# One gated unit of the second half moved into quads 16 to 18, and the first blocks of attention's output fetched a quad later

## The chip, the cores and the metric

The kernel runs on one core of one Trainium2 chip. The metric is the device time of one execution in microseconds, the median over several runs. Engines are named as in the profile: PE multiplies matrices (PEld is its loading of weights), DVE, ACT and POOL are the vector, scalar and general-purpose engines, and SP issues DMAs only. POOL and ACT issue DMAs too; each of the three has a DMA queue of its own, and 16 DMA engines serve them all.

## The reference, cut to what matters

The input x has 2048 rows of 640 features. The result mixes two branches of it with a gate g per row:

```
g   = sigmoid((x * gate_w).sum(-1))
a   = attention with a compressive memory(x) @ wo          # branch A
b   = (silu(x @ w1) * (x @ w3)) @ w2                       # branch B, inner width 1728
out = g * a + (1 - g) * b
```

Branch A has 32 heads of 20 features and works in 4 chunks of 512 rows. In a chunk every head computes a causal softmax of q k' times v, and beside it reads a memory M (sums of phi(k)' v over the earlier chunks) as phi(q) M / (phi(q) z + 1e-6). Both are mixed per head with sigmoid(beta), and the memory is updated. All is float32; the kernel splits float32 into two parts, so that one product takes three matmuls.

## The kernel before, in words

There are two streams of work for PE, and the Python code that writes the program lays one into the other. PE's order is that of the code; the other engines' order is chosen by the framework's scheduler, except where `here(...)` pins an instruction.

The first stream is attention (`attention`, L752 on). A quad is four heads of one chunk; there are 32, eight to a chunk, numbered 0 to 31, and quads 16 to 23 belong to chunk 2. The time of one quad is cut into 40 slots. Each quad has two visits. The big visit, at slot 5, does the first scores of the new quad (`s_fill`, tiles s, L590), the transposed scores of the quad before it (`t_fill`, tiles t, L623, whose exponentials ACT writes into P, L629) and the product with v of the quad two back (`pv_quad`, tile o, L643). The small visit, at slot 17, does the rest of s and t. In time, "visit O16" below is the big visit in which the o tile of quad 16 is made.

Before t can be computed for a quad, the maximum of each score row is needed: DVE takes the maxima of s (L597), ACT and DVE split them and transpose them (`max_rows`, L608), and two DMAs on ACT's queue write them into two rows of the quad's operand (tile mr into qk, L611). They are issued some slots after the small visit, and the t matmuls of the next big visit wait for them.

The second stream is everything else, in jobs: projections q, k and v of a chunk, reads of the memory (nd, L340), gated units (`ffn_up`, g and u, L262, 15 matmuls for each of g and u and each chunk), down-projections (f, L543), and the output projection of attention (`oproj`: first `normalize`, tiles rr, gt, L717 and L722, then op, L793). Chunks 0 and 1 are the first half, A; chunks 2 and 3 the second, B. `chain`, `braid` and `weave` put jobs after and into each other. Jobs are grouped into segments, `segs`, each with an end in units of ten slots. `begin` takes the next segment and divides its cost by the slots left until its end; the main loop deals out that much of it in each slot, and more of it just ahead of a visit while PSUM banks are held. A segment that is used up early lets the next one begin.

Three things around the change depend on the order. `load_memory` (L705, tile gm) issues four DMAs on POOL's queue that bring back what the memory read stored; it reuses the large buffer in which phi(q) of chunk 2 lies, so for chunk 1 it can only start when the last nd matmul of chunk 2 has read that. `load_pair` (L567, tile qk) issues DMAs on POOL's queue for the next quad's q and k. `o_load` (L690, L692, tile oall) issues DMAs on SP's queue that bring attention's output back, in five blocks of 128 features; `OUT` says after which quad of a chunk which blocks are fetched. PSUM has 8 banks, which `bank_tile` hands out in turn, so that a visit may have to wait until DVE or ACT has read what stood in a bank.

The lines that matter for the time of dealing are these:

```
end, seg = segs.pop(0)
n = end * 10 + LEAD - slots
return [end, (d for _, g in seg for d in g), sum(c for c, _ in seg) * 1e3 / n]
```

Of the kernel before, what the change touches and what calls it, by code (L numbers as in the profile page):

```python
# [18 lines left out]
S, D, H, DH, NSEG, L = 2048, 640, 32, 20, 4, 512  # L19
# [9 lines left out]
NP, AGE = 3, 4  # L29
LAG = 5  # L30
EARLY = range(2, 6)
OUT = {4: (0,), 5: (1,), 6: (2, 3)}
TOP = 1.0e10
HEADS = [(128 * b // DH, min(H - 1, (128 * b + 127) // DH)) for b in range(KB)]
PSEG = ((0, 512), (512, 384), (1024, 256), (896, 128))
# [3 lines left out]
def gated_mix(ctx: ExitStack, tc: tile.TileContext, xT, wqk, wv, w13, w2, w2h, wo, beta, out):  # L39
# [110 lines left out]
    def big_tile(name, dt=F32):  # L150
        return sp.tile([P, 4 * H * VE], dt, tag="big", name=name, bufs=1)
# [174 lines left out]
    def memory_read(c):  # L326
        pq = big.pop(("q", c))[:, :KB * L].rearrange("p (b n) -> p b n", b=KB)
        for qb in range(4):
            for hf in range(2):
                gm = f_tile(f"gm{c}_{qb}_{hf}")[:, :320]  # L330
                ps = bank_tile(f"nd{c}_{qb}_{hf}")
                nd = ps[:, :16 * VE].rearrange("p (h e) -> p h e", e=VE)
                todo = []
                for b in range(KB):
                    a0, a1 = HEADS[b]
                    u0, u1 = max(a0, 16 * hf), min(a1, 16 * hf + 15)
                    if u0 <= u1:
                        todo.append((b, a0, u0, u1))
                for n, (b, a0, u0, u1) in enumerate(todo):
                    nc.tensor.matmul(nd[:, u0 - 16 * hf:u1 - 16 * hf + 1, :],  # L340
                                     pq[:, b, qb * P:(qb + 1) * P],
                                     Ms[c - 1, b][:, u0 - a0:u1 - a0 + 1, :],
                                     start=n == 0, stop=n == len(todo) - 1, skip_group_check=True)
                r = sp.tile([P, 16], F32, tag="r16", name="nd_r")
                nc.vector.scalar_tensor_tensor(r, nd[:, :, DH], 1e-6, gH[:, 16 * hf:16 * hf + 16], op0=ALU.add, op1=ALU.mult)
                nc.vector.reciprocal(r, r)
                nc.vector.scalar_tensor_tensor(
                    gm.rearrange("p (h e) -> p h e", e=DH), nd[:, :, :DH], gate[:, c, 1, qb:qb + 1],
                    r.unsqueeze(2).broadcast_to([P, 16, DH]), op0=ALU.mult, op1=ALU.mult)
                store_later(gd[c][:, qb, 320 * hf:320 * hf + 320], gm, ("g", c, qb), n=2)  # L350
                yield 700
# [102 lines left out]
    def job_read(c):  # L454
        return 5.6, memory_read(c)
# [5 lines left out]
    def job_q(cs, mb, alloc={}):  # L461
        i = w_add(wqk[mb], D)
        return [(3.5, q_block(c, mb, i, alloc.get(c))) for c in cs]

    def job_q2(cs, mb, alloc={}):

        i = w_add(wqk[mb], D)
        j = w_add(wqk[mb + 1], D)
        return [(3.5, q_block(c, m, k, alloc.get(c), j if c == cs[-1] and m > mb else i))
                for c in cs for m, k in ((mb, i), (mb + 1, j))]  # L470
# [14 lines left out]
    def plan_down(js):  # L485
        return [w_add(w2[j] if j < NF else w2h, D) for j in js]
# [41 lines left out]
    def ffn_down(cs, js, idx, last=()):  # L528
        first = js[0] == 0
        w2s = [w_get(i, idx[0]) for i in idx]  # L530
        for c in cs:
            if c in last:
                load_share(c)
            if first:
                accs[c] = slot(f"acc{c}")[:, :KB * L].rearrange("p (b n) -> p b n", b=KB)
            for fb in range(KB):
                ps = bank_tile(f"f{c}_{js[0]}_{fb}", 1300 if len(js) > 2 else 690)
                ms = []
                for j, w in zip(js, w2s):
                    for a, b in (PASSES if j < NF else ((0, 0), (0, 1))):  # L540
                        ms.append((w[:, b, fb * P:(fb + 1) * P], hts[c, j][:, a, :]))
                for n, (w, h) in enumerate(ms):
                    nc.tensor.matmul(ps, w, h, start=n == 0, stop=n == len(ms) - 1)  # L543
                    if n % 3 == 2 and n < len(ms) - 1:
                        yield 699.0 if n == 2 and len(ms) > 5 else 699
                filled()
                dst = accs[c][:, fb]
                if first:
                    nc.scalar.copy(dst, ps)
                elif c not in last:  # L550
                    nc.vector.tensor_add(dst, ps, dst)  # L551
                else:
                    finish(c, fb, ps, (c, fb) == (NSEG - 1, KB - 1))
                yield 699 if len(ms) % 3 == 0 else 466
# [83 lines left out]
    def pv_quad(p):  # L638
# [11 lines left out]
        q = p // 2 % 8  # L650
        for b in OUT.get(q, ()):
            after(8, o_load, c, b)
# [47 lines left out]
    def load_memory(c):  # L700

        assert ("g", c, 3) in stored
        gms[c] = big_tile(f"gm{c}", FR)[:, :KB * L].rearrange("p (b n) -> p b n", b=KB)
        for qb in range(4):
            here(nc.gpsimd.dma_start(gms[c].bitcast(F32)[:, :, qb * P:(qb + 1) * P],  # L705
                                     gd[c][:, qb].rearrange("p (b n) -> p b n", b=KB)))
            yield 1
# [24 lines left out]
    def after(n, f, *a):  # L732
        soon.append([n, f, a])
# [77 lines left out]
    def job_up(cs, j):  # L811
        return (4 if j < NF else 2) * 3.5, ffn_up(cs, j, plan_up([j])[0])
# [6 lines left out]
    def job_down(cs, g, last=()):  # L819
        return 2.32 * sum(3 if j < NF else 2 for j in GROUPS[g]), ffn_down(cs, GROUPS[g], plan_down(GROUPS[g]), last)  # L820

    def jobs_up(cs, g):
        return [job_up(cs, j) for j in GROUPS[g]]
# [4 lines left out]
    def jobs_oproj(c):  # L828
        a, b = oproj(c, plan_wo())
        return (3.5, a), (17.5, b)  # L830
# [10 lines left out]
    def chain(jobs):  # L841
        return sum(c for c, _ in jobs), (y for _, g in jobs for y in g)

    def braid(a, b, every, skip=0, rest=True):

        def gen():
            n = 0
            for y in a[1]:
                yield y
                n += not isinstance(y, float)  # L850
                if n > skip and (n - skip) % every == 0:
                    z = next(b[1], None)
                    if z is not None:
                        yield z
            if rest:
                yield from b[1]
        return a[0] + b[0], gen()

    A, B = (0, 1), (2, 3)
# [15 lines left out]
    segs = []  # L875

    seg = job_q2(A, 3)
# [5 lines left out]
    o1, o2 = jobs_oproj(0)  # L883
    seg = [d, braid(chain(u), o1, 5), o2] + [job_up(A, j) for j in GROUPS[3][2:]] + [job_down(A, 3)]
# [9 lines left out]
    seg = job_q(B, 1) + job_q(B, 2)  # L894
    q = job_q2(B, 3)
    r = job_read(2)
    up = [job_up(B, 0), job_up(B, 1)]
    seg += q[:2] + [braid(chain(q[2:]), r, 2, 7, False)]
    r = 0.6 * r[0], r[1]
    seg += [braid(braid(up[0], r, 2), (0, load_memory(1)), 3, 10)]  # L900
    segs.append((2 * H + LAG + 2, seg))
    up.append(job_up(B, 2))
    o1, o2 = jobs_oproj(1)
    seg = [braid(chain(up[1:]), o1, 4, 11), braid(o2, job_read(3), 3, 1), job_down(B, 0), braid(chain(jobs_up(B, 1)), (0, load_memory(2)), 5)]
    segs.append((3 * H + LAG + 1, seg))
    d = job_down(B, 1)
    u = [job_up(B, j) for j in GROUPS[2][:2]]
    o1, o2 = jobs_oproj(2)
    seg = [d, braid(chain(u), o1, 5), o2] + [job_up(B, j) for j in GROUPS[2][2:]]
# [3 lines left out]
    o1, o2 = jobs_oproj(3)  # L913
# [118 lines left out]
```

## Time and profile before

| | us |
|---|---|
| median of 3 runs | 1116.88 (1114.8 to 1116.93) |
| profiled execution, its time | 1114.77 |
| profiled execution, its span | 1113.0 |
| PE busy | 1096.1 |
| PE mean granted clock over the span | 0.997 |
| DVE, POOL, ACT busy | 587.6, 494.9, 461.9 |

The profile covers one execution, so sums are made against 1114.77; 1.8 us of it lie outside the span. Busy shares are averages over the span. What matters here is a stretch from about 603 to 815 us, quads 13 to 22. There the o matmuls of the visits O13 to O22 start at 603.0, 634.2, 657.8, 685.7, 707.9, 729.8, 749.7, 772.2, 794.7 and 814.8 us; each of these is a PE row of the timeline with the tile o. A row of the timeline gives the start, the duration, the engine, the line, the operation with its tiles, and in brackets the idle time before it with what ended it. Successive matmuls overlap, so a group's cost is the distance between starts.

### The profile page before, as it was taken

The page shows a single profiled execution, that of the slowest core. Times are in us where ns is not written, and L with a number is a line of the kernel's source. Part 1 is how long each engine was busy: PE and PEld are TensorE (multiplying, and loading weights), DVE is VectorE, ACT ScalarE, POOL GpSimd, SP SyncE. Part 2 cuts the span into 40 slices and gives each one's busy share as a digit, 9 for nine tenths or more (in the row PEclk, how much of TensorE's full clock was granted, in tenths as well). Part 3 has the DMA queues.
Part 4 walks back from the last instruction along what each step waited for, and adds up shares of the span by engine and source line. Part 5 has one row for each costly group of instructions (what it writes and reads, how often), then busy time and mean ns, then how long its engine had stood idle before and what let it go on. Part 6 is the DMA issues. An engine that isn't in the chain of part 4 may idle for free.

```text
span 1113.0 us, 17965 instructions
## 1 busy us (share of the span) xinstructions
PE 1096.1 (98%) x6285; PEld 853.2 (77%) x6285; DVE 587.6 (53%) x1708; ACT 461.9 (41%) x952; POOL 494.9 (44%) x603
## 2 busy tenths in 40 slices
PE   9999999999999999999999998999999999999997
PEld 6988877777777777788977776777777777777786
DVE  5032564355565554466253676874557765651545
ACT  6265344454243233265265644435544443344130
POOL 5053445355355254253253436544744445354132
PEclk9999999999999999999999999999999999999999
DMA  8265943335265134446285867454754434432123
GB/s 320 94 232 201 276 116 93 82 89 135 58 147 125 52 84 128 118 105 188 94 270 201 300 185 175 107 161 133 177 127 109 123 83 114 101 104 76 51 59 114
DMA packets 87545, 153.20 MB, mean 138 GB/s; under 512 B 11584, under 2 KB 25184, under 8 KB 87456
## 3 DMA queue, kind: packets, MB, share of 16 engines
q1 hardware_dynamic: 63040, 106.30, 30.1%
q0 software_dynamic: 20384, 38.68, 15.7%
q10 hardware_dynamic: 4032, 7.08, 1.9%
q8 instruction: 50, 0.82, 0.3%
q14 instruction: 39, 0.32, 0.1%
HBM read 96.56 MB, written 54.54 MB: 136 GB/s over the span
## 4 chain that ended last, share of the span: by engine, by line
PE 87%; issue 3%; DMA 3%; DVE 3%; ACT 2%; POOL 2%; SPq 0%; ACTq 0%; DVEq 0%; POOLq 0%
PE g L262 16%; PE f L543 16%; PE u L262 15%; PE v L373 6%; PE k L262 6%; PE q L262 6%; PE o L643 6%; PE s L590 4%; PE op L793 4%; PE t L623 3%; PE pm L437 1%; PE nd L340 1%; DMA qk<-mr 1%; ACT P L629 1%; POOL W L117 1%
## 5 line engine op out<-in xcount | busy, mean ns | idle before, releaser
L117 POOL TENSOR_TENSOR W<-wr,W 128x640 fp32r<-128x640 f32 (+1 forms) x126 | 198.0, 1578 | 280.8 <-ACT W L116 218.7
L597 DVE CUSTOM_DVE_ANT_0 junk<-s,mask 128x256 bf16<-128x256 f32 (+3 forms) x512 | 250.4, 489 | 110.5 <-PE s L590 78.1
L629 ACT ACTIVATE P<-t 128x512 f32<-128x512 f32 (+1 forms) x384 | 172.2, 538 | 144.8 <-PE t L623 115.9
L262 PE MATMUL g<-X,W 128*128 128x512 f32 x840 | 208.6, 398 | 1.6 <-ACT P L629 1.6
L262 PE MATMUL u<-X,W 128*128 128x512 f32 x780 | 197.1, 399 | 0.0
L543 PE MATMUL f<-ht,W 128*128 128x512 f32 x820 | 196.4, 396 | 0.0
L262 PEld LDWEIGHTS g<-X,W 128*128 128x128 f32 x840 | 156.1, 188 | 38.3 <-ACT P L629 1.8
L633 POOL TENSOR_SCALAR_AFFINE_SELECT P<-P 128x256 f32<-128x256 f32 x192 | 93.2, 495 | 198.3 <-ACT P L629 198.1
L543 PEld LDWEIGHTS f<-ht,W 128*128 128x128 f32 x820 | 152.7, 188 | 36.4
L262 PEld LDWEIGHTS u<-X,W 128*128 128x128 f32 x780 | 143.8, 188 | 34.5 <-ACT P L629 0.3
L116 ACT CAST W<-wr 128x640 fp32r<-128x640 f32 (+1 forms) x133 | 95.7, 729 | 128.5 <-PE u L262 28.6
L117 POOL TENSOR_TENSOR ht<-ft,ht 128x512 fp32r<-128x512 f32 x52 | 68.4, 1316 | 82.6 <-ACT ht L116 79.1
L567 POOL DMA_DIRECT2D qk<-qkd x128 | 83.1, 651 | 2.9 <-PE t L623 1.8
L590 PE MATMUL s<-qk 60*128 60x256 f32 (+3 forms) x512 | 77.2, 345 | 1.5 <-DVE fu L503 1.0
L262 PE MATMUL k<-X,W 128*128 128x512 f32 x300 | 77.0, 403 | 0.7 <-ACT P L629 0.7
L643 PE MATMUL o<-P,vg 128*32 128x512 f32 (+3 forms) x1024 | 77.2, 443 | 0.2
L262 PE MATMUL q<-X,W 128*128 128x512 f32 x300 | 74.1, 402 | 1.0 <-ACT X L116 0.6
L503 DVE SCALAR_TENSOR_TENSOR fu<-ft,g 128x512 f32<-128x512 f32 x52 | 35.7, 686 | 70.1 <-ACT ft L502 69.8
L373 PE MATMUL v<-W,X 128*128 128x320 f32 (+1 forms) x480 | 71.6, 311 | 0.4 <-ACT P L629 0.4
L373 PEld LDWEIGHTS v<-W,X 128*128 128x128 f32 x480 | 71.0, 189 | 0.8 <-ACT P L629 0.6
L262 PEld LDWEIGHTS q<-X,W 128*128 128x128 f32 x300 | 55.9, 189 | 16.3 <-DVE X L117 1.1
L551 DVE TENSOR_TENSOR acc<-f,acc 128x512 f32<-128x512 f32 x65 | 44.7, 689 | 44.8 <-PE f L543 44.6
(117 smaller groups left out, 1123.0 us busy)
## 6 DMA issues: line engine op xcount, KB each, us to landing
qk<-qkd POOLq DMA_DIRECT2D x128, 240.0 KB, 4.3
wr<-in_w_dram SPq DMA_DIRECT2D x80, 320.0 KB
qkd<-qs SPq DMA_DIRECT2D x20, 512.0 KB
qkd<-ks SPq DMA_DIRECT2D x20, 512.0 KB
od<-oq SPq DMA_DIRECT2D x32, 256.0 KB
wr<-in_wo_dram SPq DMA_DIRECT2D x20, 320.0 KB
vg<-vd SPq DMA_DIRECT2D x16, 336.0 KB
xr<-in_xT_dram SPq DMA_DIRECT2D x20, 256.0 KB
```

The costliest lines, as they stand in the source:

```text
L116: pin(nc.scalar.copy(dst[:, 0], src))
L117: (lo or nc.gpsimd.tensor_sub)(dst[:, 1], src, dst[:, 0].bitcast(F32))
L262: nc.tensor.matmul(ps, w[:, a, kb * P:(kb + 1) * P], x[:, b, kb, :], start=n == 0, stop=n == 14)
L373: nc.tensor.matmul(ps[:, :n1 - n0], x[:, a, kb, lb * P:(lb + 1) * P], wvt[kb][:, b, n0:n1], start=n == 0, stop=n == 14)
L543: nc.tensor.matmul(ps, w, h, start=n == 0, stop=n == len(ms) - 1)
L551: nc.vector.tensor_add(dst, ps, dst)
L567: here(nc.gpsimd.dma_start(t[64 * i:64 * i + RH], qkd[c][RH * (h + i):RH * (h + i + 1)]))
L590: nc.tensor.matmul(ps[i][:, o:o + w], q[:, qb * P:(qb + 1) * P], key[:, :w], start=n == 0, stop=n == len(todo) - 1, skip_group_check=True)
L597: nc.vector.tensor_tensor_reduce(out=junk[:, :w], in0=ps[i][:, o:o + w], in1=mask[:, L - w:], scale=1.0, scalar=-3.0e38, op0=ALU.add, op1= ...
L629: last["exp"] = nc.scalar.activation(pairs[2 * m + k]["P"][:, i, o:o + n], ps[i][:, b:b + n], AF.Exp, scale=SCALE)
L633: nc.gpsimd.affine_select(d, d, pattern=[[0, 2], [0, n], [1, P]], base=0, channel_multiplier=-1, compare_op=ALU.is_ge, fill=0.0)
L643: nc.tensor.matmul(ps[32 * i:32 * i + 32, kb * P:], heads[2 * p + i]["v"][:, kb], pairs[p + i // 2]["P"][:, i % 2, o:o + n], start=kb == 0 ...
```

## The change

The first gated unit that was handed to the fourth segment, `up[1]` (unit 1 of the second half, for chunks 2 and 3), is appended to the third segment, whose end moves from `2 * H + LAG + 2` = 71 to `2 * H + 11` = 75 units of ten slots, that is from quad 17.75 to quad 18.75. The fourth segment keeps unit 2 alone, and braids the normalization of chunk 1 into it after every third step from the start, where it was after every fourth step, the first eleven left out, of units 1 and 2 together. `OUT` now fetches blocks 0 and 1 of every chunk after its quad 5, where block 0 was fetched after quad 4.

```
-OUT = {4: (0,), 5: (1,), 6: (2, 3)}
+OUT = {5: (0, 1), 6: (2, 3)}
...
     seg += [braid(braid(up[0], r, 2), (0, load_memory(1)), 3, 10)]
-    segs.append((2 * H + LAG + 2, seg))
+    seg.append(up[1])
+    segs.append((2 * H + 11, seg))
     up.append(job_up(B, 2))
     o1, o2 = jobs_oproj(1)
-    seg = [braid(chain(up[1:]), o1, 4, 11), braid(o2, job_read(3), 3, 1), job_down(B, 0), braid(chain(jobs_up(B, 1)), (0, load_memory(2)), 5)]
+    seg = [braid(up[2], o1, 3), braid(o2, job_read(3), 3, 1), job_down(B, 0), braid(chain(jobs_up(B, 1)), (0, load_memory(2)), 5)]
     segs.append((3 * H + LAG + 1, seg))
```

In the program that this makes, PE has the same matmuls in another order, between the visits O13 and O22 only. Counting matmuls of the second stream between visits (a g, u or q group has 15):

| between | before | after |
|---|---|---|
| O13 and O14, after the small visit | 69 of q | 54 of q |
| O14 and O15, ahead of the small visit | 21 of q | 21 of q |
| O14 and O15, after it | q 6, then nd, q, g, u | q 21, then the same |
| O15 and O16, ahead of the small visit | nd, g 6, nd, g 6, nd, g 3, u 6 | nd, g 6 |
| O15 and O16, after it | u 9, g 15, u 15, g 15 | nd, g 6, nd, g 3, u 15, g 15, u 15 |
| O16 and O17, ahead of the small visit | rr and gt of block 0, u 9 | g 15, u 6 |
| O16 and O17, after it | u 6, g 15, u 15, with blocks 1 to 3 | u 9, g 15, u 15, with blocks 0 to 2 |
| O17 and O18, ahead of the small visit | g 15, u 6, with block 4 | g 15, u 6, with blocks 3 and 4 |
| O18 and O19, ahead of the small visit | nd, op 9 | nd, op 6 |
| O20 and O21, after the small visit | f 12, g 15, u 15, g 15 | f 12, g 15, u 15 |
| O21 and O22, ahead of the small visit | u 6 | g 15, u 6 |

On POOL's queue the order between O15 and O16 was two gm loads, two qk loads, two gm loads, two qk loads; it becomes four qk loads and then four gm loads. On DVE, ACT and SP the instructions are the same ones too, and follow PE's new order.

## The prediction

> **What bounds the kernel now.** I read the page first: engines, granted clock, then the chain that ended last.
>
> ```profile
> PE 1096.1 (98%) x6285; PEld 853.2 (77%) x6285; DVE 587.6 (53%) x1708; ACT 461.9 (41%) x952; POOL 494.9 (44%) x603
> PE 87%; issue 3%; DMA 3%; DVE 3%; ACT 2%; POOL 2%; SPq 0%; ACTq 0%; DVEq 0%; POOLq 0%
> ```
>
> PE bounds it. The change leaves PE its matmuls, so the time moves only by PE's waits and by its clock. The view of waits, for PE, has thirteen lines; these lie in or near the stretch that is reordered:
>
> ```profile
> PE t L623 <- DMA qk<-mr: 2.2, 1, 2.2
> PE g L262 <- ACT P L629: 1.6, 1, 1.6
> ...
> PE s L590 <- DVE m L597: 0.5, 1, 0.5
> PE gt L722 <- DVE m L597: 0.5, 1, 0.5
> ```
>
> The timeline of PE shows where (all rows below that name PE are of it):
>
> ```profile
> 633.61 0.63 PE L623 MATMUL t<-qk 62*128 62x512 f32 x6
> ...
> 657.83 2.36 PE L643 MATMUL o<-P,vg 128*32 128x512 f32 x32
> ...
> 660.93 0.57 PE L590 MATMUL s<-qk 60*128 60x384 f32 x4
> ...
> 663.65 0.85 PE L340 MATMUL nd<-Ms,pq 128*128 128x147 f32 x6
> ...
> 668.67 0.50 PE L590 MATMUL s<-qk 60*128 60x256 f32 x4
> ...
> 671.83 3.65 PE L262 MATMUL g<-X,W 128*128 128x512 f32 x15
> 675.31 3.63 PE L262 MATMUL u<-X,W 128*128 128x512 f32 x15
> ...
> 682.36 0.50 PE L590 MATMUL s<-qk 60*128 60x512 f32 x2
> 685.07 0.73 PE L623 MATMUL t<-qk 62*128 62x512 f32 x6 [2.21 <-DMA qk<-mr]
> 685.73 3.98 PE L643 MATMUL o<-P,vg 128*32 128x512 f32 x32
> ...
> 695.33 0.50 PE L590 MATMUL s<-qk 60*128 60x384 f32 x4 [0.52 <-DVE m L597]
> ...
> 697.42 0.66 PE L722 MATMUL gt<-ident,gm 128*128 128x128 f32 x4 [0.46 <-DVE m L597]
> ...
> 707.32 0.63 PE L623 MATMUL t<-qk 62*128 62x512 f32 x6
> ...
> 732.90 0.58 PE L590 MATMUL s<-qk 60*128 60x384 f32 x4
> ...
> 736.42 0.50 PE L590 MATMUL s<-qk 60*128 60x256 f32 x4
> ```
>
> At 685.07 PE waits 2.21 us for the row maxima of quad 17. Right behind it the same 32 o matmuls take 3.98 us that take 2.36 in visit O15. That is the clock, as windows show (span, then busy time of five engines, granted clock, DMA share, GB/s):
>
> ```profile
> 616.00:624.00 8.00, 8.00 (x44) 6.44 (x43) 6.80 (x25) 5.24 (x11) 4.28 (x6) 1.00 1.16 326
> 624.00:630.00 6.00, 6.00 (x28) 4.84 (x27) 2.77 (x4) 2.98 (x7) 1.57 (x1) 1.00 1.00 381
> 668.00:676.00 8.00, 8.00 (x43) 6.25 (x42) 5.64 (x23) 3.36 (x8) 7.96 (x11) 1.00 1.10 246
> 676.00:685.00 9.00, 6.87 (x30) 5.07 (x28) 6.45 (x13) 2.54 (x4) 4.25 (x4) 1.00 0.89 216
> 685.00:700.00 15.00, 13.88 (x93) 8.72 (x94) 9.70 (x32) 7.14 (x16) 6.97 (x12) 0.89 0.40 101
> 930.00:945.00 15.00, 13.42 (x98) 9.42 (x98) 8.91 (x30) 7.90 (x16) 10.80 (x14) 1.00 0.59 163
> ```
>
> The clock falls to 0.89 over 685 to 700, and stays 1.00 around the wait of 1.6 us (g on P), which lies in 930 to 945. The DMA engines are full (1.10, 0.89) just when the maxima travel. ACT's timeline has the issues of three quads' maxima (15, 17, 18), the chain of waits the transfer of the second:
>
> ```profile
> 623.46 1.06 ACTq L611 DMA_DIRECT2D qk<-mr  x2
> ...
> 675.59 1.08 ACTq L611 DMA_DIRECT2D qk<-mr  x2
> ...
> 704.14 1.05 ACTq L611 DMA_DIRECT2D qk<-mr  x2
> ```
> ```profile
> 676.14 8.79 DMA qk<-mr
> ```
>
> From the end of an issuing pair, quad 17's maxima took 684.93 - 676.67 = 8.3 us; quad 18's at most 707.32 - 705.19 = 2.1, since t did not wait.
>
> **What the change takes away.** (S1) The 2.21 us. (S2) The half clock, 3.98 - 2.36 = 1.62 us. (S3) 0.52 + 0.46 = 0.98 us: between O16 and its small visit DVE had rr and gt to read beside the scores; now 21 matmuls of g and u stand there, and normalization is spread behind it. Together 4.81 us, provided that quad 17's maxima come in time (A3).
>
> **What it adds.** A matmul of 512 columns costs (675.31 - 671.83) / 15 = 0.232 us, so a group of 15 is 3.48.
>
> (A1) Visit O14 comes 3.48 us earlier, its first t at 630.13 in place of 633.61, while the small visit ahead of it and the issue of quad 15's maxima stay. Allowed from issue to t: 633.61 - 624.52 = 9.1 us before, 5.6 after. Their transfer isn't shown, as nobody waited. By the rows of quads 18 and 17 it is between 2.1 and 8.3; the queues are as full as for 17 (1.16, 1.00) but move more, 326 to 381 GB/s, so I take the middle, 5.2. Block 0 of oall is now fetched here, one SP row ahead of it:
>
> ```profile
> 615.47 0.79 SPq L690 DMA_DIRECT2D oall<-od  x1
> ```
>
> That block is 128 rows of 2 KB, 256 KB, 0.8 us at 326 GB/s, in a queue that is not empty until the maxima go, so 6.0 us: a wait of 0.4. Bounds: 0, and 8.3 + 0.8 - 5.6 = 3.5. Its two more issues on SP (about 1.1 us) delay the stores of q behind them; nobody reads these within the quad.
>
> (A2) Between O15 and O16 the small visit starts at 663.65, where nd stands now, not at 668.67. Its last s tile takes a bank in which the last s of the big visit stands. DVE's timeline has that reader, and the one between O18 and O19:
>
> ```profile
> 664.81 0.28 DVE L597 CUSTOM_DVE_ANT_0 junk<-s,mask 128x128 bf16<-128x128 f32 x1
> ...
> 713.11 0.69 DVE L718 TENSOR_TENSOR on<-oall,rr 128x512 f32<-128x512 f32 x1
> 713.71 0.28 DVE L597 CUSTOM_DVE_ANT_0 junk<-s,mask 128x128 bf16<-128x128 f32 x1
> ...
> 736.43 0.28 DVE L597 CUSTOM_DVE_ANT_0 junk<-s,mask 128x128 bf16<-128x128 f32 x1
> ```
>
> DVE is done at 665.09. PE comes to that matmul 0.65 us into the visit, at 664.30 (s then t then s at the starts of other visits). Wait: 0.85 us with the semaphore. Bounds 0.5 and 1.0, since both ends are rows.
>
> (A5) In the same way the small visit after O18 comes three op, 0.70 us, earlier: 735.72, its last s at 736.37, DVE done at 736.71. Wait 0.35, 0 to 0.5.
>
> (A3) Quad 17. O16's t, due at 682.70 but for the wait (s plus 0.34), is due at 682.70 - 3.48 + 0.85 = 680.07. The maxima: after the small visit DVE has eight score reads, two nd eliminations and the product of g ahead of the split, some 6 us from 665.1; then split, transposes and the issue, ending near 672.9, in place of 676.67. Allowed: 7.2 us, in place of 6.0, of which it took 8.3. POOL's timeline has the traffic that fills the queues:
>
> ```profile
> 666.94 1.82 POOL L705 DMA_DIRECT2D gm<-gd  x2 [3.61 <-PE nd L340]
> 668.75 1.36 POOL L567 DMA_DIRECT2D qk<-qkd  x2
> 670.10 1.80 POOL L705 DMA_DIRECT2D gm<-gd  x2
> ```
>
> POOL stood 3.61 us on nd, with the qk loads queued behind. Now the qk loads go first, near 663.4 and 666.4, into queues that were idle; gm waits for the later nd and is issued from 668.8 to 672.4 (four at 0.9), the weight split behind it moving from 671.92 to 672.4, not needed for a quad. All POOL loads are thus out 3.4 us earlier, the maxima 3.8 earlier, but a good part of the bytes has left by then. I take a wait of 0.5, with the clock full as after the 1.6 us; bounds 0, and 2.3 (8.3 + 1.2 for four gm at a stretch, less 7.2) with the clock lost again, 3.9.
>
> (A4) Between O16 and O18 five blocks of normalization now stand closer behind one another, and the small visit after O17 takes banks that rr of block 4 and g have left. Stepping through DVE from the end of the scores at 0.60 us an operation (713.11 to 713.71), I find DVE some 0.5 us behind PE at O17 and the bank free 0.1 after PE wants it. I take 0.2; bounds 0, and 1.1 (0.69 for each operation).
>
> (A6) Quads 19, 22 and 23 have less than 1 us between maxima and t; O21 comes 3.48 us earlier, with block 0's fetch moved away from quad 22 to 23. I take 0.2, 0 to 1.5. Elsewhere the fetch moves 256 KB by one quad, where t has several us to spare: nothing, and if that cover went, as in A1. Output blocks are needed two quads later at the earliest.
>
> **Sum.** -4.81 + 0.4 + 0.85 + 0.35 + 0.5 + 0.2 + 0.2 = -2.3 us. The profiled execution would go from 1114.77 to 1112.5; the median of the runs before lies 2.1 above it, and I carry the difference over: 1116.88 - 2.3 = 1114.6 us. About 0.2%, 2.2 us, is what a measurement of this kernel can tell from no change; the forecast lies on that edge, on the faster side.
>
> **Two rules weighed.** In the row the clock went after a wait of 2.21 us. The Trainium skill, TensorE: Matmul & The Clock Gate, "Why this matters for your kernels", asks for gaps under about 3 us, one idle window: by that S2 would not have happened. The row decides against it here; by the page the sum would be -0.7. In the row of 8.79 us a small transfer crossed full queues no faster than the rest. The Trainium skill, DMA: Bandwidth & Descriptors, "Queues, rings and completion order", says that each engine takes turns between queues packet by packet: by that the maxima on their own queue would pass the backlog, A1 and A3 would vanish, and the sum would be -3.2, which is most of R3 below. The row speaks against it, though the page's turns may still shorten a wait.
>
> **Rivals.** (R1) Quad 17's maxima are as late as before, A3 at its upper end: -4.81 + 2.0 + 3.9 = +1.1, 1118.0. For it: the same bytes, issued with the maxima. Against it: 1.2 us more allowed, half the bytes earlier. (R2, the other side) Quad 15's maxima are late: from 5.6 us to landing PE waits at 630, up to 3.5, and past about 2 us of wait the clock halves, 1.6: -2.3 - 0.4 + 3.5 + 1.6 = +2.4, 1119.3. It ends slower than the bound if the transfer takes 8.9 us, block 0 included, close above quad 17's 8.3. (R3) The maxima pass the other transfers, as quad 18's did within 2.1 us, and the banks are free in A4 and A6; only A2 and A5 stay: -4.81 + 1.2 = -3.6, 1113.3. Against it: the row of 8.79 us. (R4) A4 and A6 reach their upper ends: -2.3 + 2.2 = -0.1, 1116.8; the change only trades waits.
>
> **Chances.** Forecast 0.40 (0.27 of it faster, 0.13 within, as it lies on the edge); R3 0.18, faster; R1 0.16 (0.10 within, 0.06 slower); R2 0.13, slower; R4 0.13, within. Faster 0.45, within 0.2% 0.36, slower 0.19. Range 1111 (R3 and a run at the level of the profiled execution) to 1119 (short of R2's end).
>
> **What would show it.** Right: no wait on mr over 1 us at O14 and O16; the o matmuls of O16 in about 2.4 us and the clock at 1.00; no 0.5 us waits on DVE between O16 and O17; new waits on the maxima's reads (DVE junk or m) of about 0.8 us in the small visit between O15 and O16 and of 0.4 in that after O18; O14 and O16 some 3 us earlier than before, O15 about level, O17 and all behind it 2 to 4 us earlier. Wrong: a wait on mr of over 1.5 us at O14 or O16, a second fall of the clock, or waits of over 1 us in a small visit.

## The result and the profile after

| | before | after |
|---|---|---|
| median of 20 runs each | 1116.39 us | 1112.91 us |
| lowest to highest | 1113.13 to 1117.57 | 1110.56 to 1118.47 |
| profiled execution | 1114.77 us | 1111.06 us |
| its span | 1113.0 us | 1109.3 us |
| its granted clock, mean | 0.997 | 1.000 |

The changed kernel takes 0.9977 of the time before, with an interval of 0.9968 to 0.9986: 3.5 us less by the medians, 3.7 us less by the profiled executions. It is faster, as forecast; the forecast, 1114.6 us, lies 1.7 us above the measured median.

The engines on the profile page of the changed kernel (busy time, share of the span, instructions):

```profile
PE 1094.8 (99%) x6285; PEld 853.0 (77%) x6285; DVE 588.4 (53%) x1708; ACT 461.3 (42%) x952; POOL 493.8 (45%) x603
```

PE still bounds it, with the same 6285 matmuls. The view of waits, for PE, of the changed kernel (us in total, times, longest):

```profile
PE g L262 <- ACT P L629: 1.8, 1, 1.8
...
PE nd L340 <- ACT P L629: 1.1, 1, 1.1
...
PE t L623 <- DMA qk<-mr: 0.6, 1, 0.6
```

The 2.2 us on quad 17's maxima are 0.6 now, and the two waits of 0.5 us on DVE's m are gone from the list. PE's timeline shows each place that the prediction named (start, busy time, then the idle time before it in brackets):

```profile
630.14 0.63 PE L623 MATMUL t<-qk 62*128 62x512 f32 x6
...
664.28 0.95 PE L590 MATMUL s<-qk 60*128 60x384 f32 x4
...
680.44 0.73 PE L623 MATMUL t<-qk 62*128 62x512 f32 x6 [0.61 <-DMA qk<-mr]
681.11 2.36 PE L643 MATMUL o<-P,vg 128*32 128x512 f32 x32
...
690.34 0.45 PE L590 MATMUL s<-qk 60*128 60x384 f32 x4
...
706.06 0.93 PE L590 MATMUL s<-qk 60*128 60x384 f32 x4
...
732.45 0.96 PE L590 MATMUL s<-qk 60*128 60x384 f32 x4
```

Visit O14 (630.14) has no wait. O16 waits 0.61 us, and its 32 o matmuls take 2.36 us where they took 3.98. The s rows at 664.28, 706.06 and 732.45 are longer than undisturbed ones (0.45 at 690.34 for a small visit, 0.57 for the big one at 706.06, by the row of the same kind before): these are the waits for banks, which lie inside a group and so show as its length. The windows of the changed kernel (span, busy time of PE, PEld, DVE, ACT and POOL, granted clock, DMA share, GB/s):

```profile
665.00:675.00 10.00, 10.00 (x51) 8.31 (x50) 8.44 (x31) 3.21 (x8) 8.36 (x10) 1.00 1.11 288
675.00:685.00 10.00, 9.39 (x73) 6.28 (x72) 6.65 (x14) 4.18 (x9) 3.90 (x5) 1.00 0.46 139
685.00:700.00 15.00, 15.00 (x77) 11.72 (x77) 10.20 (x37) 6.23 (x15) 8.98 (x11) 1.00 0.48 128
```

The clock, 0.89 over 685 to 700 before, is 1.00, and PE is busy for all of these 15 us, where it was for 13.88. The DMA engines are as full as before (1.11) until 675, but less than half busy from then on (0.46): quad 17's maxima land at 672.64 + 7.66 = 680.30 us (the row stands under run 6), where they landed at 684.93.

Where the time went is read from the starts of the o matmuls:

| visit | before | after | difference |
|---|---|---|---|
| O13 | 603.0 | 602.9 | -0.1 |
| O14 | 634.2 | 630.7 | -3.5 |
| O15 | 657.8 | 657.8 | 0 |
| O16 | 685.7 | 681.1 | -4.6 |
| O17 | 707.9 | 703.0 | -4.9 |
| O18 | 729.8 | 725.9 | -3.9 |
| O22 | 814.8 | 811.0 | -3.8 |
| O31 | 1028.6 | 1024.9 | -3.7 |

One group of 3.48 us is ahead of O14 before and behind it after, so -3.5 there is the moved work alone. From O15 to O16 the next group is moved out as well: -3.48 - 2.21 + 0.61 (the maxima) + 0.50 (the s row at 664.28) = -4.58, and -4.6 is what the table has. By O17 that group has been done as well. The -4.9 there still leaves out one block of normalization, some 0.7 us, which now stands behind O17, and the wait of 0.36 us that follows (A4 below); so it is -3.9 at O18. All that is won is won between O15 and O17, and the end keeps it.

### The profile page after: what moved, and what is told of

It is laid out like the page before. It is cut to its first block, busy times and chain, and to the rows that moved or that the text cites. A ratio compares the mean times of both kernels' runs of the same rounds, so it can differ in the third digit from the quotient of the medians.

```text
span 1109.3 us, 17962 instructions
## 1 busy us (share of the span) xinstructions
PE 1094.8 (99%) x6285; PEld 853.0 (77%) x6285; DVE 588.4 (53%) x1708; ACT 461.3 (42%) x952; POOL 493.8 (45%) x603
## 4 chain that ended last, share of the span: by engine, by line
PE 88%; DVE 4%; issue 2%; DMA 2%; ACT 2%; POOL 1%; ACTq 0%; SPq 0%; DVEq 0%; POOLq 0%
PE g L262 16%; PE f L543 16%; PE u L262 15%; PE v L373 6%; PE k L262 6%; PE q L262 6%; PE o L643 5%; PE op L793 5%; PE s L590 4%; PE t L623 3%; PE nd L340 1%; PE pm L437 1%; DVE junk L597 1%; DMA qk<-mr 1%; PE pkt L422 1%
```

## The experiments

Each kernel is compared with the kernel before on the same chip. Times are medians, ratios (with their intervals) are against the kernel before.

**1. Only the later fetches (e1_out_only).** The kernel before with one line of the change:

```diff
-OUT = {4: (0,), 5: (1,), 6: (2, 3)}
+OUT = {5: (0, 1), 6: (2, 3)}
```

> The kernel before, with the new OUT alone (blocks 0 and 1 of attention's output fetched after quad 5). Theory (the gain comes from the new place of the gated unit: quad 17's row maxima in time, clock kept, normalization spread): no change, ratio to before 0.999 to 1.001; the wait of 2.2 us on the maxima (tile mr) at visit O16 and the half clock behind it stay. Rival (the fetch in its old place crowds the DMA engines and is what the change mends): the wait at O16 shrinks and the ratio is 0.998 or less.

Measured: 1117.16 us, 1.0007 [0.9993, 1.0021]. PE's timeline of this run:

```profile
685.40 1.22 PE L623 MATMUL t<-qk 62*128 62x512 f32 x6 [2.60 <-DMA qk<-mr]
686.55 4.49 PE L643 MATMUL o<-P,vg 128*32 128x512 f32 x32
...
696.83 0.50 PE L590 MATMUL s<-qk 60*128 60x384 f32 x4 [0.51 <-DVE m L597]
...
698.92 0.66 PE L722 MATMUL gt<-ident,gm 128*128 128x128 f32 x4 [0.46 <-DVE m L597]
```

All that the change takes away is still there: the wait on the maxima (2.60), the half clock (o in 4.49 us) and both waits on DVE. The fetches alone gain nothing.

**2. Only the new segment (e2_seg_only).** The changed kernel with the old line of `OUT`.

> The changed kernel with the old OUT: the gated unit alone is moved. Theory: the same as the whole change, ratio to before 0.997 to 0.9985, a wait on mr at O16 of 0 to 1 us, no half clock; at O14 no wait, as 256 KB less lie ahead of quad 15's maxima. Rival (both parts are needed: the old fetch of block 0 of chunk 2 comes before quad 22's maxima, which have 3.5 us less time now): a new wait of 0.5 us or more on mr at O21, ratio 0.999 or more.

Measured: 1112.14 us, 0.9972 [0.9960, 0.9985]. PE's timeline:

```profile
680.02 0.74 PE L623 MATMUL t<-qk 62*128 62x512 f32 x6 [0.37 <-DVE ft L509]
...
932.14 4.15 PE L262 MATMUL g<-X,W 128*128 128x512 f32 x10 [1.42 <-ACT P L629]
```

The segment gives the whole gain without the fetches, and no wait on the maxima appears at O21, which the rival expected; the interval of this run and that of the changed kernel overlap almost wholly. The wait at O16 is even a little shorter, 0.37 us (the row names ft, which ends just before; but in run 10, with the same order on PE, t starts at 679.05 while ft runs until 679.52, so t does not wait for ft, which leaves the maxima). The last row, far from the change, is taken up below: ten g matmuls in 4.15 us, at half clock.

**3. The gm loads later (e3_gm_late).** The kernel before, its order of matmuls kept, with GpSimd's four gm loads put later, in order to have them behind quad 17's maxima:

```diff
-    seg += [braid(braid(up[0], r, 2), (0, load_memory(1)), 3, 10)]
+    seg += [braid(up[0], r, 2)]
...
-    seg = [braid(chain(up[1:]), o1, 4, 11), ...
+    seg = [braid(braid(chain(up[1:]), (0, load_memory(1)), 1, 7), o1, 4, 15), ...
```

> The kernel before with one thing moved: the four loads of the stored memory read (gm, POOL's queue) are issued after quad 17's row maxima in place of ahead of them; PE's order is that of before. Theory (the maxima wait behind those transfers): the wait of 2.2 us on mr at O16 falls below 0.5 us and the o matmuls of O16 take 2.4 us, not 4.0; time 3 to 4 us less, ratio 0.9965 to 0.998; the 0.5 us waits on DVE before O17 stay. Rival (the maxima are late because DVE and ACT issue them late): the wait stays near 2 us, ratio 0.999 to 1.001.

Measured: 1112.7 us, 0.9977 [0.9963, 0.9991]. GpSimd's timeline, and PE's:

```profile
673.94 1.83 POOL L705 DMA_DIRECT2D gm<-gd  x2
...
681.18 1.75 POOL L705 DMA_DIRECT2D gm<-gd  x2
```
```profile
682.25 0.63 PE L623 MATMUL t<-qk 62*128 62x512 f32 x6
682.81 2.36 PE L643 MATMUL o<-P,vg 128*32 128x512 f32 x32
...
687.73 0.10 PEld L717 LDWEIGHTS <-sel 96*128 96x128 bf16 x1 [1.45 <-DMA rR<-rp]
687.76 0.38 PE L717 MATMUL rr<-rR,sel 96*128 96x512 bf16 x1 [1.27 <-ACT P L629]
...
693.70 0.55 PE L722 MATMUL gt<-ident,gm 128*128 128x128 f32 x3 [0.46 <-DVE m L597]
```

The edit did a little less and a little more than it says. The maxima are issued from 675.13, so two of the four loads, at 673.94, still go ahead of them. And as GpSimd no longer stands waiting for nd, the qk loads go out earlier too, at 662.82 and 671.10 in place of 668.75 and 674.42. With nothing of the change but this, the wait of 2.21 us is gone and the clock is kept: it was the loads on GpSimd's queue that the maxima waited behind. What part the gm and what part the qk loads had in the 2.21 us is not told apart here; run 10 moves the gm loads alone. The second wait on DVE stays, as it should. Normalization meets a new wait of 1.27 us: the row of PE names P, but the load of rr's weights ahead of it waits until the same time for rR, whose transfer is issued on SP's queue from 679.76 on, among the gm loads. That takes back a part of the gain: the time falls by 2.3 us, and not by the 3 to 4 expected.

**4. Only the looser normalization (e4_norm_late).** The kernel before with the blocks of normalization spread out behind the same group of matmuls as in the changed kernel:

```diff
-    seg = [braid(chain(up[1:]), o1, 4, 11), ...
+    seg = [braid(chain(up[1:]), o1, 3, 20), ...
```

> The kernel before with the normalization of chunk 1 alone moved to where the change has it (after every third step, from the third of unit 2 on). Theory: the two 0.5 us waits on DVE between O16 and O17 go, one of 0.4 us comes at visit O17; the wait of 2.2 us at O16 and the half clock stay; time 0.5 to 1.2 us less, ratio 0.999 to 0.9997. Rival (normalization is what most of the gain comes from): 2 us or more less, ratio 0.998 or less.

Measured: 1113.62 us, 0.9990 [0.9977, 1.0003]. PE's timeline:

```profile
685.44 0.81 PE L623 MATMUL t<-qk 62*128 62x512 f32 x6 [2.32 <-DMA qk<-mr]
686.18 3.91 PE L643 MATMUL o<-P,vg 128*32 128x512 f32 x32
...
694.89 0.45 PE L590 MATMUL s<-qk 60*128 60x384 f32 x4
...
698.38 0.60 PE L722 MATMUL gt<-ident,gm 128*128 128x128 f32 x4
```

The wait on the maxima and the half clock stay, and both waits on DVE are gone. The wait of 0.4 us expected at O17 did not come: the last s group there takes 0.56 us. The interval of the time includes no change, and the profiled execution, 1117.29 us, is longer than that of before, since it lost the clock twice more, later on (last section). So by the rows, though not by the time, what the prediction calls S3 is separate from S1 and S2, and comes from where normalization stands.

**5. More traffic ahead of the maxima, at the first attempt (e5_gm_twice).** The changed kernel, each gm load of chunk 1 issued twice (`for _ in range(2 if c == 1 else 1):` around the issue).

> The changed kernel with each of the four gm loads of chunk 1 issued twice, so that the same queue carries twice its bytes ahead of quad 17's row maxima; the matmuls and their order are unchanged, and the second copy writes the same values. Theory (the maxima's time to land is set by what the other queues still have to move): the wait on mr at O16, 0.61 us in the changed kernel, grows by more than 1.5 us, to 2 to 5 us, and the clock halves behind it as it did before the change; the time rises by 2 to 6 us, to 1115 to 1119. Rival (the maxima are late by their own issue and travel past the others): the wait at O16 stays at 0.3 to 1 us and the time at 1113, but for waits on POOL's later work. By the theory the remaining margin of the change at O16 is about nothing: any added transfer goes straight into PE's wait.

Measured: 1111.78 us, 0.9967 [0.9954, 0.9980], and no wait at O16. The experiment did not do what it says. GpSimd's timeline:

```profile
668.89 2.71 POOL L706 DMA_DIRECT2D gm<-gd  x3 [0.67 <-PE nd L340]
...
676.70 0.87 POOL L706 DMA_DIRECT2D gm<-gd  x1 [3.50 <-DMA gm<-gd]
```

Three loads go out back to back, and the fourth waits 3.50 us until a gm load has landed. (So it is not each second copy that waited for its first, as the expectation of run 6 puts it.) Only three loads were issued ahead of the maxima, from 672.35 on, not eight, and less stood before them than in the changed kernel. It tells nothing on more traffic; with one load fewer the 0.61 us was gone in this execution.

**6. More traffic, at the second attempt (e7_gm_more).** The changed kernel with a copy of 640 KB behind the first gm load, to an array that nobody reads:

```diff
             here(nc.gpsimd.dma_start(gms[c]...[:, :, qb * P:(qb + 1) * P], ...))
+            if (c, qb) == (1, 0):
+                here(nc.gpsimd.dma_start(gz, gd[c][:, :2]))
```

> The changed kernel with one more transfer: behind the first gm load of chunk 1, GpSimd issues a copy of two blocks' worth of gd (640 KB) to an array in DRAM that nobody reads. Nothing waits for it; the order of the matmuls and of GpSimd's other instructions is unchanged. (The loads issued twice did not put more bytes ahead of the maxima, since each second copy waited for the landing of the first.) Theory (quad 17's maxima land when the other queues are through with their bytes): the wait on mr at O16 grows from 0.6 us to between 2 and 5 us, the clock may halve behind it, and the time rises by 1.5 to 6 us, to 1114.5 to 1119. Rival (the maxima pass the other queues, and 0.6 us comes of their own way): the wait stays at 0.3 to 1 us and the time within 0.7 us of 1112.9.

Measured: 1113.74 us, 0.9980 [0.9970, 0.9990]. GpSimd's timeline, PE's, and the transfer in the chain of waits between 660 and 690:

```profile
669.22 0.58 POOL L709 DMA_DIRECT2D gz<-gd  x1
```
```profile
680.93 0.74 PE L624 MATMUL t<-qk 62*128 62x512 f32 x6 [1.38 <-DMA qk<-mr]
```
```profile
672.36 8.43 DMA qk<-mr
```

In the changed kernel the same transfer stands in that chain as

```profile
672.64 7.66 DMA qk<-mr
```

The wait is 1.38 us in place of 0.61, less than the 2 to 5 that the theory gave. At 288 GB/s, the rate of that stretch in the changed kernel, 640 KB take 2.2 us, and the copy had landed by 677.1 us, so its bytes did go ahead of the maxima, whose transfer took 0.77 us longer. These are single executions, though. Five profiles with the same order on PE and the same four loads ahead of the maxima (the changed kernel and runs 2, 7, 8 and 9) have waits of 0.61, 0.37, 0.74, 1.04 and 0.86 us at O16, and t starts 7.0 to 7.7 us after the end of the maxima's issue; here it starts 680.93 - 672.88 = 8.05 us after it. So the added bytes cost the maxima 0.4 to 1.0 us, between a fifth and a half of their own 2.2: the maxima wait with the other queues' bytes, but not behind all of them. Neither the full theory nor the rival holds.

**7. Waits on purpose in a quiet stretch (e6_waits).** The changed kernel, the maxima of quads 26 to 30 issued later:

```diff
-            after(4, lambda d=dst, ...
+            after({52: 18, 54: 20, 56: 21, 58: 22, 60: 23}.get(p, 4), lambda d=dst, ...
```

> The changed kernel with the row maxima of quads 26 to 30 issued later by PE's count, by 14, 16, 17, 18 and 19 slots more, so that PE meets waits of about 0 to 3 us at five visits in a stretch with little DMA traffic. Theory A (a wait must reach about 2 us to halve the clock): only waits from 2 us up are followed by t and o matmuls at about twice their duration. Theory B (what counts is how the wait lies against a fixed beat, besides its length): of waits between 1.2 and 2.2 us some are followed by a half clock and some are not, with no order by length. Theory C (only waits of 3 us and more): none under 3 us is. Each halved stretch costs 1.5 to 1.8 us over the wait itself. The time is 5 to 12 us above the changed kernel's by all three.

Measured: 1112.93 us in its one time. The only wait on mr in its list is quad 17's, 0.7 us: the maxima still came in time at all five visits, so none of the three theories was tested where it was meant to be. The waits on P that it has all the same are used below.

**8 and 9. The next wait (v_a_late, v_e2_late).** The largest wait left in the changed kernel is that of 1.80 us on P at 932.86. ACT's timeline of the changed kernel:

```profile
931.59 0.72 ACT L116 CAST W<-wr 128x640 fp32r<-128x640 f32 x1 [1.43 <-DMA wr<-in_w_dram]
932.22 2.18 ACT L629 ACTIVATE P<-t 128x512 f32<-128x512 f32 x6
```

A copy of a weight tile waits for its load, and the six exponentials that PE needs are queued behind it. The edit puts the splits of four tiles behind the last exponentials issued:

```diff
+LATE = (91, 92, 112, 113)
...
-        split(..., pin=behind(after))
+        split(..., pin=behind(last["exp"] if k in LATE else after))
```

> The changed kernel with the splits of four weight tiles (91, 92, 112, 113) put behind the last exponentials issued before them, so that ACT's copy of tile 113, which waits for its DMA, no longer stands ahead of the six exponentials of visit O27; PE's order is unchanged. Theory (PE's wait of 1.80 us on P at 932.86 comes from that copy): the wait falls below 0.4 us and the time by 1.2 to 1.8 us, to 1111.1 to 1111.7 by medians; the wait of 1.1 us on P at 751 stays. Rival (what the copy delays moves to its reader, the group of matmuls that takes tile 113): a new wait on the weight of about 1 us, and the time is within 0.5 us of the changed kernel's 1112.9.

> The same splits put back in the kernel that has the new segment but the old times of the fetches of oall (1112.1 by its median). There the wait on P at 932 was 1.42 us and the clock halved for 3.4 us behind it. Theory (both come from ACT's copy of tile 113): wait and half clock go, 1.2 + 1.7 = about 2.9 us, to 1109 to 1110. Rival (as above, the reader of the tile waits in place of P): 1111.5 to 1112.5.

Measured: 1109.67 us, 0.9955 [0.9941, 0.9970], with the change; 1109.81 us, 0.9955 [0.9940, 0.9969], with the new segment alone. ACT's timeline in the first:

```profile
930.72 2.19 ACT L631 ACTIVATE P<-t 128x512 f32<-128x512 f32 x6 [0.15 <-PE t L625]
```

The exponentials no longer wait, PE's wait on P there is gone in both, and no wait for a weight replaces it: the theory held, and the first gained more than the 1.2 to 1.8 us expected: 3.2 us by the medians, 2.5 by the ratios, which set each kernel against the one before on its own chip. In six of the nine profiles here that have that wait a half clock followed it, and that can no longer happen; the gain beyond the wait itself is put down to this, which is an argument and not shown. The fetches of oall make no difference here either.

**10. Both together (v_b3).** The kernel of run 8, with the four gm loads moved on GpSimd's queue behind the next two weight splits:

```diff
-    seg += [braid(braid(up[0], r, 2), (0, load_memory(1)), 3, 10)]
-    seg.append(up[1])
+    seg += [braid(up[0], r, 2)]
+    seg.append(braid(up[1], (0, load_memory(1)), 1, 3))
```

> The changed kernel with the four weight splits behind the exponentials, as in v_a_late, and with the four gm loads of chunk 1 moved on GpSimd's queue behind the next two weight splits, some 5 us, so that quad 17's maxima leave first; PE's order is unchanged. Theory: the wait at O16, 1.04 us in v_a_late, falls below 0.2 us, and gm still lands before the transposes gt that read it, as these come only behind O16: 0.5 to 1 us less than v_a_late's 1109.7, so 1108.7 to 1109.2. Rival (as in e3, where rr then waited 1.27 us): a new wait of 0.5 to 1.5 us at rr or gt behind O16 gives the gain back: 1109.3 to 1110.2.

Measured: 1108.12 us, 0.9937 [0.9923, 0.9950], the fastest of all and better than both kernels of this case. GpSimd's and PE's timelines:

```profile
676.20 3.54 POOL L707 DMA_DIRECT2D gm<-gd  x4
```
```profile
679.05 0.63 PE L625 MATMUL t<-qk 62*128 62x512 f32 x6
679.62 2.36 PE L645 MATMUL o<-P,vg 128*32 128x512 f32 x32
```

The loads leave 7.6 us later than in the changed kernel, behind the maxima, whose issue ends at 672.49; the qk loads stay where they were. t follows s without a wait, and neither rr nor gt, which reads what gm brings, has one in the list. Against run 8 this is 1.5 us by the medians and 2.0 by the ratios, where the theory had 0.5 to 1; the two intervals overlap, so the time alone does not settle it, and the wait does. In this order of matmuls there was room that the kernel before did not have: the first rr stands at 693.52 here, and at 687.76 in run 3, where it had to wait for rR.

## Why the prediction was right

- **S1 (2.21 us on the maxima of quad 17)**: gone but for A3's 0.61. The cause, the loads of GpSimd's queue that travel with the maxima, is shown by run 3, where the loads move and PE's order does not and the wait goes, and by run 10, where the gm loads alone move and what was left of it goes. Run 6, where more bytes go along, points the same way with a small number.
- **S2 (half clock, 1.62 us)**: gone, 3.98 to 2.36. That it comes of the wait is shown by runs 1 and 4, which kept both, and by run 3, which lost both with PE's order kept. The limit of about 2 us that the prediction read out of two waits, 1.6 us without a half clock and 2.21 with, does not hold: in the last section a wait of 1.32 us cost the clock and one of 1.80 did not. It did no harm here, as the wait that is left, 0.61 us, is shorter than any that cost the clock.
- **S3 (0.98 us of waits on DVE)**: gone, with 0.1 us more than the waits themselves, as the rows behind them became shorter too (s from 0.50 to 0.45, gt from 0.66 to 0.60). The rows of run 4 show it alone; its time does not.
- **A1 (0.4, up to 3.5, on quad 15's maxima)**: nothing. The second issue ends at 624.76 + 0.52 = 625.28, and t starts at 630.14 without a wait, so the maxima took at most 4.9 us; the prediction had taken 5.2 and added 0.8 for block 0. R2, the rival on the slower side, fell with it.
- **A2 (0.85)**: 0.95 - 0.45 = 0.50, at the lower bound. PE did meet the bank still being read, but DVE was done earlier, at 664.39 + 0.28 = 664.67 and not at 665.09. In DVE's timeline of before a pause of 0.50 us stood ahead of the visit's second read, and after it is 0.15:

```profile
662.08 0.69 DVE L597 CUSTOM_DVE_ANT_0 junk<-s,mask 128x512 bf16<-128x512 f32 x1 [0.50 <-DVE m L597]
```
```profile
661.44 0.08 DVE L597 DVE_READ_ACCUMULATOR2_ANT m<- 128x1 f32 x1
661.67 0.69 DVE L597 CUSTOM_DVE_ANT_0 junk<-s,mask 128x512 bf16<-128x512 f32 x1
...
664.39 0.28 DVE L597 CUSTOM_DVE_ANT_0 junk<-s,mask 128x128 bf16<-128x128 f32 x1
```

The mistake was to carry DVE's time over from the trace of before. Why the pause became shorter was not tried.
- **A3 (0.5)**: 0.61, with the clock kept, as taken. R1 fell. The times of issue came out nearly as worked out: gm from 668.56 to 672.14, where the prediction had 668.8 to 672.4, and the maxima until 673.15, where it had 672.9. That the wait itself fits so well is in part luck, as 0.5 was taken from between 0 and 2.3, and the same loads gave 0.37 to 1.04 us in five profiles. The margin there is small: with one gm load fewer there was no wait (run 5), and with 640 KB more it was 1.38 us (run 6).
- **A4 (0.2)**: 0.93 - 0.57 = 0.36, but at the big visit behind O17, where the prediction had the small one. An addition of normalization stands there in DVE's queue ahead of the copy of o and of the scores' reads (705.14 to 705.83 in DVE's timeline of the changed kernel):

```profile
705.14 0.69 DVE L725 TENSOR_TENSOR oall<-on,gm 128x512 fp32r<-128x512 f32 x1
705.75 0.69 DVE L647 COPY oq<-o 128x512 f32<-128x512 f32 x1
706.35 0.68 DVE L597 CUSTOM_DVE_ANT_0 junk<-s,mask 128x512 bf16<-128x512 f32 x1
```

DVE being behind, as the prediction had it, and nearly the size were right; the place was wrong. Run 4, with normalization spread in much the same way, does not have this wait, so what it takes besides was not found.
- **A5 (0.35)**: 0.96 - 0.45 = 0.51, at the upper bound.
- **A6 (0.2)**: no new wait at O19, O22 or O23. The small visit behind O21 even gained 0.34: its s row, 0.79 before, is 0.45.

The sum with measured sizes: -2.21 - 1.7 (S2, all that a 3.41 us stretch at half clock loses) - 1.1 + 0.50 + 0.61 + 0.36 + 0.51 - 0.34 = -3.4, and the waits on P, 0.1 less at 751 and 0.2 more at 933, make it -3.3. The spans differ by 3.7; some 0.4 us are spread over rows too small to name. So the direction and most of the steps were right. The change was forecast as -2.3 us and is -3.5 by the medians, -3.7 by the profiles. Of that gap about 1.0 us is A1, A2 and A6 taken too dear and S2 and S3 a little too cheap, less what A3, A4 and A5 cost more than forecast; the last 0.4 is not traced. The forecast time was 1.7 us too high, and 0.5 us of this is the level from which it started: 1116.88 was a median of three runs, and the median of 20 is 1116.39.

R3 gave 1113.3, which is nearer to the measured time than the forecast, but its mechanism was not what happened: the maxima did not pass the other transfers, they still waited 0.61 us. On the rule of the Trainium skill weighed there (DMA: Bandwidth & Descriptors, "Queues, rings and completion order": engines take turns between the queues), run 6 gives a number for how far it could help: 640 KB more on another queue delayed a transfer of 16 KB by 0.4 to 1.0 us, and not by the 2.2 us that they take at the measured rate. Turns would fit that, but the runs do not show them; what the runs do show is that the small transfer is not independent of a full queue.

## What to carry to other kernels

A small transfer that a busy engine waits for should be issued ahead of the large ones that nobody needs yet, even if its queue is its own; in run 3 moving the loads of one queue was worth as much as the whole change to the order of the matmuls (0.9977 both). A copy that waits for a load should not stand in an engine's queue ahead of work that the bounding engine waits for. And when a group of matmuls is dealt across a boundary, the waits that it brings are to be priced with the reader's moved times, not with its old ones.

## What the runs showed that was not expected

A wait much shorter than 2.21 us can cost the clock, and whether it does depends on when it falls. The windows of run 4 around three waits (2.32, 1.32 and 1.85 us), cut at the edges of the stretches at half clock:

```profile
682.53:685.94 3.41, 1.09 (x8) 0.71 (x8) 1.91 (x5) 1.32 (x2) 1.53 (x1) 1.00 0.34 92
685.94:689.35 3.41, 3.41 (x24) 1.00 (x25) 0.00 (x0) 2.07 (x4) 0.84 (x2) 0.50 0.37 101
750.80:754.21 3.41, 2.09 (x27) 1.50 (x20) 2.60 (x7) 2.80 (x7) 2.85 (x3) 1.00 0.54 156
754.21:757.62 3.41, 3.41 (x12) 2.83 (x11) 1.65 (x9) 1.81 (x5) 3.39 (x6) 0.50 0.77 249
935.12:938.53 3.41, 1.56 (x10) 1.14 (x8) 2.81 (x12) 2.54 (x7) 2.79 (x3) 1.00 0.52 175
938.53:941.94 3.41, 3.41 (x10) 2.64 (x9) 0.00 (x0) 0.99 (x2) 2.92 (x4) 0.50 0.34 99
```

Each time the clock is 0.50 for 3.41 us, and the three stretches begin 68.27 and 184.32 us apart, 20 and 54 times 3.4133. Between stretches of one execution the distances were whole multiples of that in all the runs that had more than one. So the clock looks to be judged on a beat of 3.41 us that runs through, by what PE did in the beat before, and a wait that is cut by a beat's edge counts in two parts. The kernel before shows that case. Its wait of 1.58 us ended at 936.54, and its beats, counted from the half clock at 686.31, have an edge at 935.48:

```profile
935.48:938.89 3.41, 2.35 (x10) 1.96 (x11) 2.14 (x10) 3.05 (x8) 2.56 (x4) 1.00 0.54 167
938.89:942.30 3.41, 3.41 (x23) 2.61 (x23) 0.84 (x2) 0.86 (x2) 2.82 (x3) 1.00 0.39 98
```

Its wait fell 0.5 us in one beat and 1.06 in the next, PE was busy 2.35 us of that, and the clock stayed. In these profiles, the last beats of the kernel left out, every beat in which PE was busy for 2.15 us or more was followed by a full clock, but for the one that was itself at half clock in run 1, and most of those with less by a half one (1.42 us of wait in run 2, 1.56 in run 3, 1.78 in run 5). Four with less were not: 1.92 us busy in the changed kernel,

```profile
931.37:934.78 3.41, 1.92 (x8) 1.61 (x9) 2.35 (x10) 3.04 (x8) 2.81 (x4) 1.00 0.52 172
934.78:938.19 3.41, 3.41 (x18) 2.52 (x18) 0.69 (x1) 1.10 (x2) 2.94 (x4) 1.00 0.49 117
```

and waits of 1.5 and 1.6 us on P in runs 7 and 9 and of 1.38 us on the maxima in run 6. In the first three PE had run mostly matmuls over all 128 rows, in the halved ones largely s and t, over 60 and 62 rows. Counting s and t by the share of rows that they use parts the two kinds near 1.4 us with one exception, but that is a fit to a dozen beats and not shown. The Trainium skill, TensorE: Matmul & The Clock Gate, "Why this matters for your kernels", has gaps up to about 3 us as safe; by these rows a wait of 1.32 us inside one beat is not, and the measurement decides.

This also bears on the spread of the times. Of the 20 runs of the changed kernel, the four with the lowest time, 1110.56 to 1111.06, had a mean clock of 0.999 or 1.000, the two with the highest, 1116.42 and 1118.47, one of 0.994 and 0.995; one halved beat costs 0.0015 of the mean and 1.7 us. The kernel of run 10, which has one wait over 1.1 us left behind its start, had five times within 1.8 us. That the spread is such beats is argued from this, not shown.
